# Retention in quarter-array blocks, heads kept at rows h//4, and a new place for the retention blocks and the sums in a fused retention and gated MLP kernel

## The chip, the cores and the metric

The kernel runs on one core of one Trainium2 chip. A core has a matrix engine (TensorE, "PE" in the profile; its weight loads are "PEld"), a vector engine (VectorE, "DVE"), a scalar engine (ScalarE, "ACT"), a general engine (GpSimd, "POOL") and a queue engine (SyncE, "SP") that issues most DMAs. Matmul results go to PSUM, which this kernel divides by names: `a`, `b` and `m` are two banks each, `n` and `st` one bank each, eight in all. A bank holds 2 KB for each of the 128 partitions.

The metric is the device time of one execution in microseconds, lower is better. Times are compared as the median of several runs, and the profile shows one of those executions.

## What is computed

Eight sequences of 576 positions, eight heads of 64. A retention block (attention without softmax, with a decay per head) is followed by an MLP with the activation h cos(h). All inputs and the output are float32; the kernel computes its matmuls in bfloat16 and sums in float32.

```
scale = 1.0 / np.sqrt(D_)
scores = scale * np.matmul(q, k.transpose(0, 1, 3, 2))
gamma = 1.0 - 2.0 ** (-5.0 - np.arange(H, dtype=np.float32))
Dmat = np.where(rel >= 0, gamma[:, None, None] ** rel[None, :, :], 0.0)
attn_out = np.matmul(scores * Dmat[None, :, :, :], v)

x = attn_out.transpose(0, 2, 1, 3).reshape(B * S, H * D)   # 4608 x 512
h = x @ w_in                                               # 512 -> 2048
out = (h * np.cos(h)) @ w_out                              # 2048 -> 512
```

## The kernel before

**Row blocks and tiles.** The 4608 token rows are 36 row blocks g of 128. Nine row blocks hold two sequences (1152 = 2 x 576 rows), so g % 9 says where a block lies: 0 starts a sequence, 4 (`MIX`) has the end of one sequence in its first 64 rows and the start of the next in the others, 8 ends one. The MLP works on ten tiles n of 512, 256, 256 and then seven times 512 rows. Tiles n = 3 (`S7`) to 9 (`last`) are the ones in which the second matmul is done by seven products instead of eight.

**Retention of a row block.** The decay splits into a factor for q rows and one for k rows, so `prep` (L128) multiplies q and k by tables (`gq`, `gk`, made by exponentials at the start) and casts v, mostly on POOL. The results are transposed, by TensorE for the first row blocks and by DMA later. Then, for eight heads written as pairs (head 2*hg + he, with he choosing one half of 128 partitions):

- `scores` (L176): eight matmuls of k rows against q rows, contraction 64, output 128 rows, into bank `a` or `b`, he in one or the other of its two banks; DVE multiplies by a causal mask and writes `ret` in bfloat16 (L192).
- `states` (L229): the sum over the block of k times v, eight matmuls of 128x64 per block, in two column halves; DVE adds the running state (`s`, L265, or a copy at a sequence start, L263), and `copy` (L251) casts it into one of four blocks `sb` (L256), block-diagonal 128x128 tiles with the two heads of a pair on the diagonal and zeros elsewhere.
- `attn_out` (L271): for two row blocks at a time, first the carried part, four full 128x128 matmuls of `sb` against q for each block (L283; not for a block that starts a sequence, and 64 columns for MIX), then the block's own part, eight matmuls of 128x64 of v against `ret` (L296); ScalarE casts the sum from bank `m` into the activations `xT` (L308).
- `state` and the single-block calls of `attn_out` do the same for the first row blocks.

**The MLP of a tile.** `mm1` (L312) makes h in eight blocks i = 0 to 7 in banks `a`, `b`, `m`; ScalarE computes cos(h) as a shifted sine (L331), DVE multiplies (L332) into `gT`. For n < 3, `mm2` accumulates 16 matmuls (L340) for each 128 rows. For n >= 3, gT and w_out are seen as 2 x 2 quarters and `mm2_seven` (L474) computes seven products of quarter sums, in the order 3, 4, 5, 2, 1, 7, 6 (called M3, M4 and so on here), each of 16 matmuls with 256 columns (L455). The sums of gT quarters (gs5, gs2, gs1, gs7, gs6) are made by `g_sum` (L383), each in two halves of four of eight blocks, on DVE or POOL; a POOL sum that follows a DVE one waits for it ("port free"). Sums of weight quarters are made once by `w_sums`. `sums_after` (L414) says after which mm1 block each sum is issued: for most tiles the first halves after block 3, the second after block 7.

M3, M5, M1 and M6 use bank `n`, M4, M2 and M7 bank `st`: M5 accumulates on M3 and M2 on M4, after the earlier value has been read out. The output quarters are combined by DVE (L484), collected in `pend` and issued by `flush` at the next product.

**The order.** Everything is in a hand-written order (`manual_schedule`): each engine executes its own instructions strictly in the order in which the code issues them, and semaphores are put in between from the tiles that they read and write. Retention work of later row blocks is put between the products: `unit7` (L711) issues, for two row blocks, states (bank `b`), the pending combination (`then`), attn_out (bank `m`), scores of the next two blocks (`scores2`, banks `a` and `b`) and the sb copies on ScalarE. The table `at` (L768) says ahead of which product a unit stands: M5 and M1 in tiles 5 to 8; in tiles 3 and 4 only scores ahead of M5, and units ahead of M1 and M6. `feed` (called at every store) issues the next preparations, transposes and loads.

Of the kernel before, what the change touches and what calls it, by code (L numbers as in the profile page):

```python
# [8 lines left out]
F32 = mybir.dt.float32  # L9
# [8 lines left out]
def kernel(  # L18
# [17 lines left out]
    P = 128  # L36
# [61 lines left out]
    blocks4 = [consts.tile([P, HG, P], BF16, tag=f"sb{x}", name=f"sb{x}") for x in range(4)]  # L98

    tiles = {}  # L100

# [26 lines left out]
    def prep(g, early=False):  # L128
# [6 lines left out]
        tq = gq[:, c, :].unsqueeze(2).to_broadcast([P, H, D])  # L135
        tk = gk[:, c, :].unsqueeze(2).to_broadcast([P, H, D])
        if not early:
            fq = tiles.pop(("fq", g))
            nc.gpsimd.tensor_tensor(out=qks[:, 0], in0=fq, in1=tq, op=ALU.mult)  # L139
        (nc.vector if g == 3 else nc.gpsimd).tensor_tensor(  # L140
            out=qks[:, 1], in0=fk, in1=tk, op=ALU.mult
        )
        if early:
            tiles["fv", g] = fv
        else:
            copy_v = nc.scalar.copy if g > starts[S7] // P + 17 else nc.gpsimd.tensor_copy
            copy_v(vb, fv)  # L147
            if c == MIX and g > PER:
                copy_v(v_odd[HP:, g // PER % 2], fv[HP:])
        qT = qT4[:, :, g * P : (g + 1) * P] if early else qkT[:, :HG, :]  # L150
# [25 lines left out]
    def scores(g, bank, idle=0):  # L176
# [3 lines left out]
        for hg in range(HG):  # L180
            for he in range(2):
                d0 = he * D
                nc.tensor.matmul(  # L183
                    ps[:, he, hg, :],
                    lhsT=qkT[d0 : d0 + D, HG + hg, :],
                    rhs=qT[d0 : d0 + D, hg, :],
                    start=True,
                    stop=True,
                )
        ret = retp.tile([P, 2, HG, P], BF16, tag="ret", name="ret")  # L190
        mask = tri_mix if g % PER == MIX else tri
        nc.vector.tensor_tensor(  # L192
            out=ret.rearrange("p a b i -> p (a b) i"),
            in0=ps.rearrange("p a b i -> p (a b) i"),
            in1=mask.unsqueeze(1).to_broadcast([P, H, P]),
            op=ALU.mult,
        )
        tiles["ret", g] = ret

    def state(g):  # L200
# [10 lines left out]
        for hg in range(HG):  # L211
# [3 lines left out]
                rhs=vs[p0:, 2 * hg : 2 * hg + 2, :].rearrange("s h d -> s (h d)"),  # L215
# [13 lines left out]
    def states(gs, bank="st"):  # L229
# [6 lines left out]
        ps = psum.tile([P, len(gs), HG, D], F32, tag=bank, name="st")  # L236
        for x, g in enumerate(gs):
            qks, vb, qkT, qT = tiles["a", g]
            vs = v_odd[:, g // PER % 2] if g % PER == MIX else vb
            for hg in range(HG):  # L240
                for he in range(2):
# [3 lines left out]
                        rhs=vs[:, 2 * hg + he, :],  # L245
                        start=(x == 0 and hg == 0),
                        stop=(x + 1 == len(gs) and hg == HG - 1),
# [3 lines left out]
        def copy(run=nc.vector.tensor_copy):  # L251
            for g in gs:
                s, sb = tiles.pop(("s32", g)), blocks4[g % 4]
                for he in range(2):
                    r = slice(he * D, he * D + D)
                    run(sb[r, :, r], s[r])  # L256
                tiles["sb", g + 1] = sb
# [13 lines left out]
    def attn_out(gs, bank, evac=nc.vector.tensor_copy):  # L271


        ps = psum.tile([P, len(gs), HG, P], F32, tag=bank, name="ov")
        for x, g in enumerate(gs):
            c = g % PER
            if c == 0:
                continue
            qT = tiles["a", g][3]
            sb = tiles.pop(("sb", g))  # L280
            n = HP if c == MIX else P
            for hg in range(HG):
                nc.tensor.matmul(  # L283
                    ps[:, x, hg, :n],
                    lhsT=sb[:, hg, :],
                    rhs=qT[:, hg, :n],
                    start=(hg == 0),
                    stop=False,
                    skip_group_check=True,
                )  # L290
        for x, g in enumerate(gs):
            vb = tiles["a", g][1]
            ret = tiles.pop(("ret", g))
            for hg in range(HG):
                for he in range(2):
                    nc.tensor.matmul(  # L296
                        ps[he * D : he * D + D, x, hg, :],
                        lhsT=vb[:, 2 * hg + he, :],
                        rhs=ret[:, he, hg, :],
                        start=(g % PER == 0 and hg == 0),  # L300
                        stop=(hg == HG - 1),
                        skip_group_check=True,
                    )
        n = max(m for m in range(len(starts)) if starts[m] <= gs[0] * P)
        if ("x", n) not in tiles:
# [3 lines left out]
            tiles["x", n][:, :, t0 : t0 + len(gs) * P].rearrange("p c (x i) -> p x c i", i=P), ps  # L309
# [73 lines left out]
    def g_sum(n, x, e0, e1):  # L383
# [9 lines left out]
        if ("gs", n, x) not in tiles:  # L393
# [4 lines left out]
        on_dve = x == 5 or (n, x) in ((S7, 1), (S7, 2)) or (n, x, e0) in (  # L398
            (last, 1, 0), (last, 2, 4), (S7 + 1, 2, 4)
# [14 lines left out]
    def sums_after(n, i):  # L414

        if n == S7:
            if i < 4:
                w_sums(3 + i % 2, i // 2 * 4, i // 2 * 4 + 4)
            if i == 6:
                g_sum(n, 5, 0, 4)  # L420
            elif i == 7:
                g_sum(n, 5, 4, E2)
                g_sum(n, 2, 0, E2)
                g_sum(n, 7, 0, 4)
        elif i in (3, 7):
            for x in (5, 2, 1, 7, 6) if n < last or i > 3 else (5, 1, 2, 7, 6):
                g_sum(n, x, i - 3, i + 1)

# [36 lines left out]
    def more_sums(n):  # L465

        if n == S7:
            g_sum(n, 7, 4, E2)
            prep_next()
            g_sum(n, 1, 0, E2)  # L470
            for e in (0, 4):
                g_sum(n, 6, e, e + 4)

    def mm2_seven(n, at):  # L474
# [21 lines left out]
        for x in (3, 4, 5, 2, 1, 7, 6):  # L496
            if x in at:
                at[x](flush)
# [326 lines left out]
```

## Time and profile before

| | us |
|---|---|
| median of 5 runs | 304.89 |
| the five runs | 303.71, 303.98, 304.89, 306.76, 309.3 |
| the profiled execution | 303.71 |
| its span, first to last instruction | 302.0 |
| mean granted TensorE clock | 0.994 |
| busy in one tile, 166.0 to 196.2 us: PE, DVE, ACT, POOL | 30.20, 21.23, 17.98, 25.06 |
| the same, 226.3 to 256.5 us | 30.20, 21.31, 16.94, 21.15 |
| busy from 134 to 152 us (tile n=4): PE, DVE, ACT, POOL | 17.07, 16.11, 6.86, 17.23 of 18.00 |

The page has, for every group of instructions, its source line, engine, operation, what it writes and reads, busy time and mean duration, then the idle time of the engine just before it and what ended that idle time. A duration of one matmul there contains its latency; because matmuls overlap, the cost of a group is read from the chain of work that ended last, in which the pieces add up to the time passed. In the timeline, a bracket at the end of a row is idle time before the row, with the instruction that ended it. Three rows of groups that the change touches, from the groups by shape (mean ns of one, idle before):

```
L242 PE MATMUL st<-vb,qks 128*64 128x64 bf16 x168 | 5.0, 198 | 0.4 <-DVE ret L192 0.4
L401 POOL TENSOR_TENSOR gs<-gT 128x1024 bf16<-128x1024 bf16 x49 | 104.8, 2174 | 44.4 <-DVE gs L401 44.4
L139 POOL TENSOR_TENSOR qks<-fq,gq 128x512 bf16<-128x512 f32 x32 | 34.6, 1082 | 39.2 <-DMA fq<-in_q_dram 35.1 <-PE o L340 4.1
```

### The profile page before, as it was taken

What the parts mean: (1) busy time and instruction counts of PE and PEld (TensorE: products, weight loads), DVE (VectorE), ACT (ScalarE), POOL (GpSimd) and SP (SyncE); (2) the same over time, 40 slices, a digit from 0 to 9 for tenths busy, and PEclk for the clock granted to TensorE, in tenths of its full rate; (3) what the DMA queues carried; (4) which work ended last, traced back from release to release, by engine and by line L of the source; (5) the groups of instructions that cost most, each with busy time, mean ns of one, the idle gap of its engine ahead of it and who ended that gap; (6) DMA issues with size and microseconds to landing.
All of it is one profiled execution on the core that took longest, in us unless ns stands there. A gap on an engine that the chain in (4) does not pass through costs nothing.

```text
span 302.0 us, 6662 instructions
## 1 busy us (share of the span) xinstructions
PE 292.1 (97%) x2761; PEld 200.7 (66%) x2761; DVE 209.5 (69%) x250; ACT 145.5 (48%) x187; POOL 199.0 (66%) x165
## 2 busy tenths in 40 slices
PE   8899999999999979998999999999999999999995
PEld 3478647758588867457754885488548854884594
DVE  6677647664689994589857874787488748835873
ACT  2656433515245352652466584648455645524620
POOL 2780067444445399989984998499849934970583
PEclk9999999999999998999999999999999999999999
DMA  7999999999989999999999997995860250022013
GB/s 207 212 210 207 203 199 210 208 252 176 233 176 213 209 213 219 226 244 194 204 242 184 247 231 143 229 210 143 171 142 2 72 139 2 0 72 69 2 35 104
DMA packets 154270, 50.23 MB, mean 166 GB/s; under 512 B 140801, under 2 KB 153217, under 8 KB 154241
## 3 DMA queue, kind: packets, MB, share of 16 engines
q1 hardware_dynamic: 150016, 45.63, 75.3%
q0 software_dynamic: 4224, 4.19, 8.4%
q8 instruction: 21, 0.34, 0.5%
q14 instruction: 9, 0.07, 0.1%
HBM read 36.70 MB, written 9.44 MB: 153 GB/s over the span
## 4 chain that ended last, share of the span: by engine, by line
PE 51%; DVE 1%; DVEq 0%; issue 0%
PE h L323 23%; PE o L455 22%; PE ov L296 2%; PE sc L183 2%; PE ov L283 2%; PE st L242 1%; DVE ret L192 1%; DVE ot L484 0%; DVEq L820 0%
## 5 line engine op out<-in xcount | busy, mean ns | idle before, releaser
L401 POOL TENSOR_TENSOR gs<-gT 128x1024 bf16<-128x1024 bf16 x49 | 104.8, 2174 | 44.4 <-DVE gs L401 44.4
L323 PE MATMUL h<-xT,w_in_sb 128*128 128x512 bf16 (+2 forms) x832 | 127.9, 313 | 0.9 <-DVE gT L332 0.4
L332 DVE TENSOR_TENSOR gT<-h,cosh 128x1024 bf16<-128x1024 f32 x72 | 87.9, 1223 | 43.6 <-ACT cosh L331 43.5
L331 ACT ACTIVATE cosh<-h,half_pi 128x1024 f32<-128x1024 f32 x72 | 80.2, 1113 | 64.7 <-PE h L323 62.7
L323 PEld LDWEIGHTS <-w_in_sb 128*128 128x128 bf16 x832 | 75.9, 98 | 50.2 <-issue 1.2
L455 PEld LDWEIGHTS <-gs 128*128 128x128 bf16 x576 | 54.7, 99 | 8.9 <-issue 0.6
L139 POOL TENSOR_TENSOR qks<-fq,gq 128x512 bf16<-128x512 f32 x32 | 34.6, 1082 | 39.2 <-DMA fq<-in_q_dram 35.1
L140 POOL TENSOR_TENSOR qks<-fk,gk 128x512 bf16<-128x512 f32 x35 | 37.3, 1066 | 10.0 <-DMA fk<-in_k_dram 9.5
L192 DVE TENSOR_TENSOR ret<-sc,tri 128x1024 bf16<-128x1024 f32 x32 | 38.0, 1219 | 3.9 <-PE sc L183 3.8
L455 PE MATMUL o<-ws,gs 128*128 128x256 bf16 (+1 forms) x352 | 40.0, 275 | 0.0
L484 DVE TENSOR_TENSOR ot<-o,ot 128x512 f32<-128x512 f32 (+2 forms) x32 | 19.7, 620 | 16.3 <-PE o L455 16.2
L340 PE MATMUL o<-w_out_sb,gT 128*128 128x512 bf16 x128 | 30.1, 380 | 0.0
L308 ACT CAST xT<-ov 128x1024 bf16<-128x1024 f32 (+1 forms) x18 | 16.5, 917 | 27.5 <-PE ov L296 27.3
L455 PE MATMUL o<-w_out_sb,gs 128*128 128x256 bf16 x224 | 25.8, 273 | 0.4 <-DVE ot L484 0.4
L455 PE MATMUL o<-w_out_sb,gT 128*128 128x256 bf16 x224 | 25.6, 273 | 0.0
L455 PEld LDWEIGHTS <-gT 128*128 128x128 bf16 x224 | 21.8, 98 | 3.9
L340 PEld LDWEIGHTS <-gT 128*128 128x128 bf16 x128 | 11.8, 98 | 12.6
L401 DVE TENSOR_TENSOR gs<-gT 128x1024 bf16<-128x1024 bf16 (+1 forms) x19 | 18.2, 974 | 0.4
L256 ACT CAST sb<-s 64x256 bf16<-64x256 f32 x40 | 16.1, 403 | 0.9 <-DVE s L263 0.4
L147 POOL CAST vb<-fv 128x512 bf16<-128x512 f32 x22 | 13.4, 610 | 3.0 <-DMA fv<-in_v_dram 2.8
L350 ACT COPY ot<-o 128x512 f32<-128x512 f32 x8 | 4.7, 589 | 17.1 <-PE o L340 17.1
L183 PEld LDWEIGHTS <-qkT 64*128 64x128 bf16 x288 | 8.2, 94 | 7.0 <-issue 3.4
(70 smaller groups left out, 178.2 us busy)
## 6 DMA issues: line engine op xcount, KB each, us to landing
out_dram<-ot SPq DMA_DIRECT2D x35, 256.0 KB, 3.4
fk<-in_k_dram SPq DMA_DIRECT2D x32, 256.0 KB, 5.0
fv<-in_v_dram SPq DMA_DIRECT2D x32, 256.0 KB, 5.2
fq<-in_q_dram SPq DMA_DIRECT2D x28, 256.0 KB, 4.4
w_in_sb<-in_moe_w_in_dram POOLq DMA_DIRECT2D x4, 512.0 KB, 8.9
w_out_sb<-in_moe_w_out_dram POOLq DMA_DIRECT2D x4, 512.0 KB, 16.3
fq<-in_q_dram SPq DMA_DIRECT2D x2, 512.0 KB, 4.3
fq<-in_q_dram SPq DMA_DIRECT2D x8, 128.0 KB, 4.1
```

What stands on the lines that cost most here:

```text
L139: nc.gpsimd.tensor_tensor(out=qks[:, 0], in0=fq, in1=tq, op=ALU.mult)
L140: (nc.vector if g == 3 else nc.gpsimd).tensor_tensor(out=qks[:, 1], in0=fk, in1=tk, op=ALU.mult)
L192: nc.vector.tensor_tensor(out=ret.rearrange("p a b i -> p (a b) i"), in0=ps.rearrange("p a b i -> p (a b) i"), in1=mask.unsqueeze(1).to_br ...
L256: run(sb[r, :, r], s[r])
L308: evac(tiles["x", n][:, :, t0 : t0 + len(gs) * P].rearrange("p c (x i) -> p x c i", i=P), ps)
L323: nc.tensor.matmul(ps[:, j, :], lhsT=w_in_sb[:, dg, (et + j) * P : (et + j + 1) * P], rhs=xT[:, dg, c0 : c0 + w], start=(dg == 0), stop=(d ...
L331: nc.scalar.activation(cosh, ps, ACTF.Sin, bias=half_pi, scale=1.0)
L332: nc.vector.tensor_mul(gT[:, et : et + m, c0 : c0 + w], ps, cosh)
L340: nc.tensor.matmul(ps, lhsT=gT[:, et, tsi * P : (tsi + 1) * P], rhs=w_out_sb[:, et, :], start=(et == 0), stop=(et == ET - 1),)
L401: i = (nc.vector if on_dve else nc.gpsimd).tensor_tensor(out=tiles["gs", n, x][:, e0:e1], in0=i0, in1=i1, op=op_)
L455: nc.tensor.matmul(dst[i], lhsT=lhs[:, e, j * P : (j + 1) * P], rhs=rhs[:, e, c0:c1], start=(x in (3, 4, 1, 7) and e == 0 and (i == 0 or l ...
L484: pend.append(lambda: nc.vector.tensor_tensor(out=out_, in0=in0, in1=in1, op=op_))
```

## The change

Heads are numbered differently inside the tiles: head h = 4*he + hg now lies at rows h//4 (the partition half he), column group hg, instead of head 2*hg + he. The products in `prep` write q and k in that order, and the first load of q is split over two queues to match. The output of attn_out is laid out as [P, 4, blocks, P] so that the row half he of a head decides its PSUM bank.

With it: the state copies become 128x64 tiles without zeros, so that the clearing of the four sb tiles falls away; the carried part is computed in matmuls of 64x64, one per head, and the own part comes ahead of it when two row blocks are done together; scores are computed in two parts of 64 output rows. A tile's first unit stands ahead of M4 instead of M5 (tiles 5 to 8), and its states go to bank `st`; those of the second, ahead of M1, to bank `n`. The second halves of the sums are issued behind the first unit's states (`late_sums`); in tiles 3 and 4 the sums have another order and other engines. The mask of a unit's second score bank can be put off behind the addition of M4.

```diff
-    blocks4 = [consts.tile([P, HG, P], BF16, ...) for x in range(4)]
+    blocks4 = [consts.tile([P, HG, D], BF16, ...) for x in range(4)]
+    def head(he, hg):
+        return he * HG + hg
...
-    def prep(g, early=False):
+    def prep(g, early=False, kv_first=False):
...
+        def scaled(eng, m, f, by):
+            eng.tensor_tensor(
+                out=qks[:, m].rearrange("p (b a) d -> p a b d", a=2),
+                in0=f.rearrange("p (a b) d -> p a b d", a=2),
+                in1=by[:, c, :].rearrange("p (a b) -> p a b", a=2).unsqueeze(3).to_broadcast(
+                    [P, 2, HG, D]
+                ),
+                op=ALU.mult,
+            )
...
-    def scores(g, bank, idle=0):
+    def scores(g, bank, idle=0, parts=1, put_off=None):
...
         for hg in range(HG):
-            for he in range(2):
-                d0 = he * D
-                nc.tensor.matmul(
-                    ps[:, he, hg, :],
-                    lhsT=qkT[d0 : d0 + D, HG + hg, :],
-                    rhs=qT[d0 : d0 + D, hg, :],
+            for i0 in range(0, P, P // parts):
+                for he in range(2):
+                    d0, i1 = he * D, i0 + P // parts
+                    nc.tensor.matmul(
+                        ps[i0:i1, he, hg, :],
+                        lhsT=qkT[d0 : d0 + D, HG + hg, i0:i1],
+                        rhs=qT[d0 : d0 + D, hg, :],
...
+        if put_off is None:
+            masked()
+        else:
+            put_off.append(masked)
...
     def states(gs, bank="st"):
...
-                for he in range(2):
-                    r = slice(he * D, he * D + D)
-                    run(sb[r, :, r], s[r])
+                run(sb, s)
...
     def attn_out(gs, bank, evac=nc.vector.tensor_copy):
+        two = len(gs) == 2
+        ps = psum.tile([P, DG, len(gs), P], F32, tag=bank, name="ov")
+        def out_of(h, x, n=P):
+            return ps[h % 2 * D : h % 2 * D + D, h // 2, x, :n]
+        def carried():
+            for h0 in (0, 2) if two else (0,):
+                for x, g in enumerate(gs):
...
+                    heads = [(he, h0 + j) for j in range(2) for he in range(2)]
...
+                    for he, hg in heads:
+                        h = head(he, hg)
+                        r = slice(he * D, he * D + D)
+                        k = r if two else slice(0, P)
+                        nc.tensor.matmul(
+                            out_of(h, x, n),
+                            lhsT=sb[k, hg, r] if sb.shape[2] == P else sb[k, hg, :],
+                            rhs=qT[k, hg, :n],
...
+        for part in (own, carried) if two else (carried, own):
+            part()
...
-        on_dve = x == 5 or (n, x) in ((S7, 1), (S7, 2)) or (n, x, e0) in (
-            (last, 1, 0), (last, 2, 4), (S7 + 1, 2, 4)
+        on_dve = x == 5 or (n, x) == (S7, 2) or (n, x, e0) in (
+            (S7, 1, 4), (last, 1, 0), (last, 2, 4)
         )
...
         if n == S7:
             if i < 4:
                 w_sums(3 + i % 2, i // 2 * 4, i // 2 * 4 + 4)
-            if i == 6:
-                g_sum(n, 5, 0, 4)
+            elif i < 6:
+                g_sum(n, 5, i % 4 * 4, i % 4 * 4 + 4)
+                if i == 5:
+                    g_sum(n, 6, 0, 4)
             elif i == 7:
-                g_sum(n, 5, 4, E2)
                 g_sum(n, 2, 0, E2)
-                g_sum(n, 7, 0, 4)
-        elif i in (3, 7):
-            for x in (5, 2, 1, 7, 6) if n < last or i > 3 else (5, 1, 2, 7, 6):
-                g_sum(n, x, i - 3, i + 1)
+                g_sum(n, 1, 4, E2)
+                g_sum(n, 1, 0, 4)
+                for e in (0, 4):
+                    g_sum(n, 7, e, e + 4)
+                prep_next(kv_first=True)
+                g_sum(n, 6, 4, E2)
+        elif n == S7 + 1 and i in (3, 7):
+            for x in (5, 2, 1):
+                g_sum(n, x, i - 3, i + 1)
+            for x in (7, 6) if i == 7 else ():
+                for e in (0, 4):
+                    g_sum(n, x, e, e + 4)
+        elif i == 3:
+            for x in (5, 2, 1, 7, 6) if n < last else (5, 1, 2, 7, 6):
+                g_sum(n, x, 0, 4)
+        elif i == 7 and n == last:
+            late_sums(n)
+    def late_sums(n):
+        for x in (5, 2, 1, 7, 6):
+            g_sum(n, x, 4, E2)
...
             elif x == 4:
-                add(u22, tiles["all", 4], u22)
+                pend.insert(0, lambda: nc.vector.tensor_tensor(
+                    out=u22, in0=tiles["all", 4], in1=u22, op=ALU.add
+                ))
...
     for h0 in (0, HG):
-        nc.sync.dma_start(
...
+        for a, queue in enumerate((nc.sync, nc.scalar)):
+            at = a * HG + h0 // 2
+            queue.dma_start(
...
-            for sb in blocks4:
-                nc.gpsimd.memset(sb, 0.0)
...
-    def scores2(g):
+    def scores2(g, put_off=None):
         if g < NG:
-            scores(g, "a")
-            scores(g + 1, "b")
+            scores(g, "a", parts=2)
+            scores(g + 1, "b", parts=2, put_off=put_off)
...
-        copy = states([g + 1, g + 2], "b")()
+        copy = states([g + 1, g + 2], bank)()
...
-                    5: lambda then: unit7(g, True, then),
-                    1: lambda then: unit7(g + 2, True, then),
+                    4: lambda then, off: unit7(g, "st", True, lambda: late_sums(n), off),
+                    1: lambda then, off: unit7(g + 2, "n", True, then),
...
-                        5: lambda then: (then(), scores2(g), more_sums(n)),
-                        1: lambda then: unit7(g, True, then),
-                        6: lambda then: unit7(g + 2, n > 3, then),
+                        5: lambda then, off: (then(), scores2(g)),
+                        1: lambda then, off: unit7(g, "n", True, then),
+                        6: lambda then, off: unit7(g + 2, "b", n > 3, then),
```

## The prediction

> **What bounds the kernel now.** I read the page's engine rows first, then the chain of work that ended last in order of time, then TensorE's waits, then the timeline around each wait. From the page:
>
> ```profile
> PE 292.1 (97%) x2761; PEld 200.7 (66%) x2761; DVE 209.5 (69%) x250; ACT 145.5 (48%) x187; POOL 199.0 (66%) x165
> PE 51%; DVE 1%; DVEq 0%; issue 0%
> ```
>
> TensorE is busy for 97% of the span, and the chain (followed back to 140 us) is TensorE almost alone. A gain must come from fewer TensorE nanoseconds or fewer TensorE waits. One whole tile (n=5) in the chain:
>
> ```profile
> 166.16 3.49 PE o L455 x32
> 169.65 0.37 PE st L242 x16
> 170.02 0.55 PE ov L283 x8
> 170.57 0.57 PE ov L296 x16
> 171.14 0.55 PE sc L183 x16
> 171.69 3.60 PE o L455 x32
> 175.29 0.37 PE st L242 x16
> ...
> 182.58 13.81 PE h L323 x64
> ...
> 205.77 0.33 PE ov L283 x4
> ```
>
> Columns: start, duration, instruction group. 32 product matmuls cost 3.49 us right after mm1 (109 ns each), but 3.60 us after the score matmuls: the change of array shape costs 0.11. In a unit the shape changes five times: full array, 128x64 (st), 128x128 (carried, L283), 128x64 (own, L296), 64x128 (scores), full array. Taking 0.10 to 0.11 off each piece leaves 0.44 us for eight carried matmuls (55 ns each), 0.46 for eight pairs of own blocks (57 ns a pair), 0.44 for eight pairs of scores (55 ns a pair), and 0.26 for eight pairs of st (32 ns a pair, 64 columns moving). So two half-array tiles do run together: a pair costs what one full matmul costs.
>
> TensorE's waits, and the timeline around them:
>
> ```profile
> PE sc L183 <- DVE s L265: 1.7, 1, 1.7
> PE o L455 <- DVE ot L484: 0.4, 1, 0.4
> PE st L242 <- DVE ret L192: 0.4, 1, 0.4
> ```
> ```profile
> 107.22 2.59 DVE L401 TENSOR_TENSOR gs<-gT 128x2048 bf16<-128x2048 bf16 x1
> ...
> 111.34 0.40 PE L183 MATMUL sc<-qkT 64*128 64x128 bf16 x8 [1.67 <-DVE s L265]
> ...
> 136.62 3.23 DVE L401 TENSOR_TENSOR gs<-gT 128x1024 bf16<-128x1024 bf16 x2
> ...
> 139.93 6.31 POOL L401 TENSOR_TENSOR gs<-gT 128x1024 bf16<-128x1024 bf16 x3 [0.63 <-DVE gs L401]
> 140.50 1.91 PE L455 MATMUL o<-w_out_sb,gs 128*128 128x256 bf16 x16 [0.43 <-DVE ot L484]
> ```
>
> All three waits are DVE running late behind gs sums, in tiles n=3 and n=4. In n=3 a 2.59 us sum stands ahead of the state additions, and the second score bank waits for them. In n=4 two sums take 3.23 us beside POOL's own.
>
> **The change part by part.** Let p be the price of a round of four quarter-array matmuls. No trace of before has such a round. From below p is 56 ns (the array is as full as with one 128-column matmul). The st pairs hint at more: four instructions (two weight loads, two matmuls) in 32 ns is 8 ns each, and a round has eight: 63 ns. From above it is 112 ns (only two run together). I take 63, the nearest row, and keep 56 and 112.
>
> (a) Carried blocks. Twelve pairs of row blocks lie in n=3 to 8. Before: seven full pairs at 0.44, three with a half-width MIX block at about 0.34 (the 0.45 rows less 0.11), two with a sequence start at 0.22 (the 0.33 row less 0.11): 4.54 us. After: four rounds for ten pairs, two for two pairs, 44 rounds: 2.77 us. Gain 1.77 (2.08 at 56).
>
> (b) Scores in two parts: twelve calls, 32 matmuls instead of 16, so eight rounds instead of eight pairs: 0.50 for 0.44. Loss 0.77 (0.10 at 56). The same array work in twice the instructions: it pays only through (c).
>
> (c) Shape changes. The new order st, own, carried, scores has the shapes 128x64, 128x64, 64x64, 64x64: three changes instead of five. Ten units with scores save two each, n=3's last saves one, n=8's last (neither states nor scores) gains one: 20 x 0.10 = 2.0 gained.
>
> (d) n=3. gs5's halves move to blocks 4 and 5; after the last cos product DVE has gs2 and half of gs1 (1.14 + 0.70, the price of such sums there), and the 2.59 us sum is gone. The 1.7 us wait goes. Late next: the states of the unit before M1 now write bank n, which M3 and M5 used, so they wait for DVE's u11 subtraction, queued behind u22's addition (0.68) and two masks (1.22 each). From 102.7 us on: 1.84 + 0.68 + 2.44 + 0.68 gives 108.3 against a want of 107.9, so 0.5 stays with the semaphore. And M4 needs the last two cos products, which two 0.7 us sums now precede; DVE is busy nine tenths there, and only the sb copies (four of 64 rows, 1.18 us, become two of 128) give some back: 0.5. Queued behind M4 are scores and M5. Net gain 0.8.
>
> (e) n=4. gs2's second half leaves DVE, so u22's addition comes some 1.5 us earlier and the waits before M2 and the first states (1.1 us with their sequencer part, plus 0.3 at 149.7) mostly go. But POOL, with six sums of 2.1 us from about 137.4, ends its last half of gs6 near 149.9, where M6 would read it near 149.3: 0.6 late, and M7's second half touches at 145.8. POOL's preparations queue behind. Gain 0.5.
>
> (f) New wait, n=5 to 8. States of the first unit write bank st, and M4 writes it next. In tile n=7 the last cos product ends at 228.82, two additions (0.89 us) end at 229.74, with 0.14 to TensorE's start (as at 111.2) 229.88. M3 ended near 227.98 and the shorter unit takes 1.72, so M4 could start at 229.70: 0.18 late, with M5 and M2 queued behind it. Three tiles with two additions: 0.55 lost. Elsewhere M4 is covered by the unit itself; were DVE another 0.5 us late, that comes on top in each of the four tiles. The gs5 half behind the additions ends near 230.6, M5's second half reads it after 232: covered. gs2's second half on POOL ends at 233.5 against a read at 234.2: covered by 0.6.
>
> (g) n=1 and 2, where attn_out comes ahead of states: five shape changes more (+0.5), carried rounds (-0.47), two score calls (+0.13): 0.15 lost.
>
> At nothing: the put-off mask (next read before M1, 1.7 us later), the half-size sb copies on ACT (0.40 each for 0.82, ACT 48% busy), the missing clears of sb (2.1 us of POOL at 19.3, then waiting for loads), and the first q loads over two queues (same bytes; ACT's two issues would cost it about 1 us, at SP's 0.5 each, ahead of an Exp that is needed at 4.7 and ended at 2.4). Without that cover each is worth its own price. SP's order behind those loads is the same, so later loads, transposes and stores move past nothing. The qks products in blocks of 64 have no row on POOL: the flat ones take 1.06 to 1.08. DVE's product over four dimensions takes 1.22 for 1024 elements, no more than a flat one, so I take no change. POOL has 9 us free in tile n=7 (21.15 of 30.2), so even 1.6 us each would be hidden there, though not in n=4.
>
> Sum: -1.77 +0.77 -2.0 -0.8 -0.5 +0.55 +0.15 = -3.6 us; at p=56, -4.6. The profiled execution took 303.71 (span 302.0, and 1.7 around it) and was the fastest of five, so it becomes 300.1. The median shown is 304.89, 1.2 higher; less 3.6 it is 301.3. I put the time at 300.6, between.
>
> **A rule against the change.** The Trainium skill, "TensorE: Matmul & The Clock Gate", section "Wait — 56ns, not 53.3ns?", says that the distance from one matmul start to the next never falls below about 25 ns, however short they are. Then a round of four costs 100 ns: (a) shrinks to 0.14, (b) costs 4.3, and the sum is +1.5 us, a slower kernel. The st row speaks against it: 16 matmuls in 0.26 us are 16 ns apart, weight loads included. The measurement decides, so 63 and not 100.
>
> **The rivals.**
>
> Quarters run two at a time (slower). A round costs 112 ns: (a) and (b) become -4.54+4.93 and +5.48, the sum +3.2, or 306.9 for the profiled execution and about 307.5 as a median. Place: scores and carried blocks of every unit from n=3 on. All 140 rounds together decide from p = 89 ns, where the sum is zero. For it: no trace shows four tiles at once. Against: rows and columns each pair freely, and the two row halves of scores and of carried blocks lie in different PSUM banks. Chance 0.1.
>
> DVE and POOL take the gain back (about the same). If M4 waits 0.5 us more in n=5 to 8, and n=3 and n=4 keep their waits, 2.0 + 1.3 go and 303.5 is left. For it: DVE at nine tenths before 103 us, POOL full in n=4. Against: in n=5 to 8 no other wait is within 0.5 us. Chance 0.22.
>
> All DVE waits go and p is 56: -4.6 -1.0 (d) -0.6 (e) -0.55 (f), or 297 profiled. Chance 0.2. The forecast itself: 0.48. That the shape changes do not fall away cannot be: the order of instructions alone gives the shapes.
>
> **How the numbers follow.** About 1% (3 us) is what a measurement of this kernel tells from no change. The forecast case lies at 1.2 to 1.5% and gives three quarters to faster, the rest to within 1%; the all-waits case is faster; the DVE case within 1%, the quarter case half and half. Faster 0.64, within 1% 0.29, slower 0.07. Range 296.8 to 304.2: from p=56 with no new wait to the DVE case as a median; the slower rival and a few tenths of the DVE case are left out.
>
> **What would show it.** Carried rows: 16 matmuls in about 0.35 us after a change, scores 32 in 0.50 to 0.55 with no change ahead of them. A tile of 30.2 us should become about 29.5. A wait of M4 (product line) on the state additions near 0.2 us; none of 1.7 us on the second score bank. Wrong if 32 scores take 0.8 us or more, or if a tile in n=5 to 8 shows waits of over 0.5 us.

## The result and the profile after

| | before | changed kernel |
|---|---|---|
| median, us (all executions) | 305.09 (301.85 to 310.59, 48) | 300.36 (298.49 to 305.25, 27) |
| ratio, 95% interval | | 0.988 (0.9854 to 0.9905) |
| profiled execution: time, span, granted clock | 303.71, 302.0, 0.994 | 303.77, 302.0, 0.989 |
| second profile of the same kernel: span, clock | 301.0, 0.994 | 297.7, 1.000 |

The changed kernel is 1.2% faster. Ratios, and medians by clock, here and below are of the fast executions alone, so 0.988 is not the quotient of the two medians (0.9845), and the profiled execution of the changed kernel is one of its slow ones. It has the same span as the one of before, so that pair says nothing until one knows where the two spend their time. The page of the changed kernel, engine row and the row of the granted clock (one digit for each fortieth of the span):

```profile
PE 289.6 (96%) x3113; PEld 197.2 (65%) x3113; DVE 209.7 (69%) x245; ACT 135.7 (45%) x167; POOL 199.4 (66%) x163
PEclk9999999999999999999999599999999999999999
```

TensorE still is the bound. The 5 stands at 166 to 173 us, in tile n=5. TensorE's timeline there, and then the stretch that follows (columns: stretch, length, then busy time and instructions of PE, PEld, DVE, ACT, POOL, then granted clock, DMA share, GB/s):

```profile
164.41 0.39 PE L195 MATMUL sc<-qkT 64*64 64x128 bf16 x16
168.57 0.64 PE L195 MATMUL sc<-qkT 64*64 64x128 bf16 x16 [3.77 <-DMA qkT<-qks]
```
```profile
168.50:173.70 5.20, 5.12 (x38) 3.67 (x39) 0.86 (x2) 0.00 (x0) 5.20 (x4) 0.50 1.29 254
```

The second score bank waits 3.77 us for a transpose by DMA, and from 1.6 us before the end of that wait TensorE runs at half clock for 6.8 us (167.0 to 173.8). A second profile, of another execution of the same kernel, has neither (span 297.7), and from here on I use it, called the second profile. In the profile of before the same kind of thing happens in tile n=3, after its wait of 1.67 us for the state additions (first fence, the products behind it; second fence, the stretch):

```profile
111.68 5.33 PE L455 MATMUL o<-ws,gs 128*128 128x256 bf16 x32
```
```profile
112.00:115.40 3.40, 3.40 (x18) 2.44 (x17) 2.39 (x3) 0.48 (x2) 3.40 (x3) 0.50 1.15 252
```

The 32 products take 5.33 us, where 3.67 is normal at full clock: 1.7 us is lost, directly behind the wait. The prediction read the wait just ahead of this row, and not the row.

Where the 4.3 us between the two spans (302.0 and 297.7) lie, from the starts of mm1 and of M3:

| stage, us | before | after | difference |
|---|---|---|---|
| up to M3 of n=3 | 100.13 | 100.20 | +0.07 |
| n=3, M3 to the next mm1 | 20.06 | 16.67 | -3.39 |
| n=4 | 31.99 | 32.21 | +0.22 |
| n=5, 6, 7, 8 | 30.23, 30.02, 30.23, 29.31 | 30.09, 29.69, 29.76, 29.09 | -0.14, -0.33, -0.47, -0.22 |
| tail, from the mm1 of n=9 | 30.04 | 29.94 | -0.10 |

Nearly all of it is n=3. Against the second profile of before (span 301.0) the other rows are the same within 0.02 us, but the first is 99.17 against 100.20: the changed kernel loses 1.0 us before n=3, and the gain between these two spans is 3.4. One unit in tile n=7 of the changed kernel, for the question whether the arrays do what was said (timeline of the first profile, whose long wait lies two tiles earlier; start, duration):

```profile
225.72 6.29 POOL L443 TENSOR_TENSOR gs<-gT 128x1024 bf16<-128x1024 bf16 x3
...
228.91 0.44 PE L266 MATMUL st<-vb,qks 128*64 128x64 bf16 x16
...
229.98 0.62 PE L195 MATMUL sc<-qkT 64*64 64x128 bf16 x32
...
230.35 2.21 DVE L443 TENSOR_TENSOR gs<-gT 128x1024 bf16<-128x1024 bf16 x1
...
230.53 1.92 PE L515 MATMUL o<-w_out_sb,gT 128*128 128x256 bf16 x16
...
232.28 1.91 PE L515 MATMUL o<-w_out_sb,gs 128*128 128x256 bf16 x16
...
233.62 0.68 DVE L557 TENSOR_TENSOR ot<-o,ot 128x512 f32<-128x512 f32 x1
...
234.35 1.91 PE L515 MATMUL o<-w_out_sb,gs 128*128 128x256 bf16 x16 [0.15 <-DVE ot L557]
```

The same places in before (timeline of n=7, where the unit stands ahead of M5; then POOL's row there, from a timeline of POOL alone):

```profile
228.85 0.80 DVE L401 TENSOR_TENSOR gs<-gT 128x1024 bf16<-128x1024 bf16 x1
...
229.83 0.44 PE L242 MATMUL st<-vb,qks 128*64 128x64 bf16 x16
...
231.88 3.67 PE L455 MATMUL o<-w_out_sb,gs 128*128 128x256 bf16 x32
```
```profile
226.96 4.67 POOL L401 TENSOR_TENSOR gs<-gT 128x1024 bf16<-128x1024 bf16 x2
```

Read the starts. From st to the product behind it the unit takes 1.62 us (228.91 to 230.53); before it took 2.05 (229.83 to 231.88). M4 does not wait. But further down stands something that the prediction had not: the gs5 half on DVE takes 2.21 us instead of 0.80, pushes the mask and the addition behind it, and M2 (234.35) starts 2.07 us after M5 (232.28), where 16 products take 1.75. TensorE's waits in the second profile (total, times, longest):

```profile
PE h L365 <- DVE gT L374: 1.7, 2, 1.3
...
PE o L515 <- DVE ot L557: 1.1, 4, 0.5
PE h L365 <- DVE xT L350: 0.7, 1, 0.7
...
PE sc L195 <- DMA qkT<-qks: 0.4, 1, 0.4
```

With the sequencer's part, M2 starts 2.41, 2.20, 2.07 and 2.07 us after M5 in n=5 to 8: 0.66, 0.45, 0.32 and 0.32 us of waits, 1.75 in four tiles. The gs5 half takes 2.56, 2.68, 2.22 and 2.22 us there.

### The profile page after: what moved, and what is told of

It is laid out like the page before. It is cut to its first block, busy times and chain, and to the rows that moved or that the text cites. A ratio compares the mean times of both kernels' runs of the same rounds, so it can differ in the third digit from the quotient of the medians.

```text
span 302.0 us, 7333 instructions
## 1 busy us (share of the span) xinstructions
PE 289.6 (96%) x3113; PEld 197.2 (65%) x3113; DVE 209.7 (69%) x245; ACT 135.7 (45%) x167; POOL 199.4 (66%) x163
## 5 line engine op out<-in xcount | busy, mean ns | idle before, releaser
L443 POOL TENSOR_TENSOR gs<-gT 128x1024 bf16<-128x1024 bf16 x51 | 106.9, 2126 | 42.9 <-DVE gs L443 42.9
L515 PE MATMUL o<-ws,gs 128*128 128x256 bf16 (+1 forms) x352 | 38.6, 268 | 0.0
L515 PE MATMUL o<-w_out_sb,gT 128*128 128x256 bf16 x224 | 28.2, 283 | 0.1
L515 PE MATMUL o<-w_out_sb,gs 128*128 128x256 bf16 x224 | 26.8, 276 | 0.6 <-DVE ot L557 0.6
L535 DVE TENSOR_TENSOR ot<-o,ot 128x512 f32<-128x512 f32 (+2 forms) x25 | 14.9, 603 | 13.5 <-PE o L515 13.4
L443 DVE TENSOR_TENSOR gs<-gT 128x1024 bf16<-128x1024 bf16 (+1 forms) x18 | 21.4, 1200 | 0.3
L195 PE MATMUL sc<-qkT 64*64 64x128 bf16 (+1 forms) x480 | 11.0, 220 | 4.7 <-DMA qkT<-qks 4.2
L195 PEld LDWEIGHTS <-qkT 64*64 64x64 bf16 (+1 forms) x512 | 9.1, 107 | 9.1 <-DMA qkT<-qks 4.5
```

What stands on the lines that cost most here:

```text
L195: nc.tensor.matmul(ps[i0:i1, he, hg, :], lhsT=qkT[d0 : d0 + D, HG + hg, i0:i1], rhs=qT[d0 : d0 + D, hg, :], start=True, stop=True,)
L443: i = (nc.vector if on_dve else nc.gpsimd).tensor_tensor(out=tiles["gs", n, x][:, e0:e1], in0=i0, in1=i1, op=op_)
L515: nc.tensor.matmul(dst[i], lhsT=lhs[:, e, j * P : (j + 1) * P], rhs=rhs[:, e, c0:c1], start=(x in (3, 4, 1, 7) and e == 0 and (i == 0 or l ...
L535: pend.append(lambda: nc.vector.tensor_tensor(out=out_, in0=in0, in1=in1, op=op_))
```

## The experiments

Ratios are to the kernel before, with 95% intervals.

**The changed kernel again**, unaltered.

> The changed kernel unaltered, for a second profile. Theory 1 (the transposes of row blocks 22 and 23 stand late in SP's queue, and the unit that now comes one product earlier in tile n=5 reaches them): the second score bank of n=5's first unit waits for a transposed tile again, between 0 and 4 us from run to run; the time is 0.985 to 0.990 of the kernel before. Theory 2 (the wait of 3.8 us in the first profile was a disturbance of that execution): no wait over 0.3 us there. In both, a carried group of 16 takes 0.35 us and M2 of n=6 to 8 waits 0.3 to 0.45 us for the addition of M4.

Measured: 299.36 us, ratio 0.9901 (0.9886 to 0.9917), span 297.7, full clock. It is the second profile above. The 3.77 us wait is absent, and SP's queue shows by how much (timelines of this profile, SP's issues and the scores that read the block):

```profile
159.90 1.39 SPq L167 DMA_TRANSPOSE qkT<-qks  x1
...
165.80 0.62 PE L195 MATMUL sc<-qkT 64*64 64x128 bf16 x32
```

The transpose is issued at 159.90 for scores at 165.80, 5.9 us later. In before it was issued at 163.10 for scores at 171.14, 8.0 us. In the first profile it was issued at 162.53, and TensorE stood ready at 164.8, only 2.3 us later: SP's queue was late there by 2.3 us at the transpose before already, and TensorE was 1.0 us earlier than here, since mm1 of n=4 had not waited. A transpose lands 4.2 to 5.0 us after its issue here. Scores now come some 5 us earlier (n=3 is shorter), the transposes come when SP's queue lets them: what was slack has become chance.

**Block 23's transpose earlier in SP's queue.**

```diff
-  ... + 4 * n + ((0, 1, 2, 4) if n else (-1, 0, 1, 4))[r]
+  ... + 4 * n + ((0, 1, 2, 4) if n > 1 else (1, 2, 2, 4) if n else (-1, 0, 1, 4))[r]
```

> In tile n=4 row blocks 22 and 23 are prepared and transposed one store earlier in SP's queue (about 6 us). Theory 1: the wait of n=5's second score bank for a transposed tile is gone or under 0.5 us, and the time falls to 0.978 to 0.985 of the kernel before, 1 to 3 us under the changed kernel, with less spread. Theory 2: the time stays within 0.3% of the changed kernel.

Measured: 299.87 us, 0.9907 (0.9883 to 0.9931), span 298.3. A miss: the edit moved the transpose past one store only (issued at 159.48), with the loads still ahead, and the unaltered kernel had no wait there in the same set of runs. It decides nothing.

**Carried blocks ahead of own**, which makes three shape changes five again.

```diff
-        for part in (own, carried) if two else (carried, own):
+        for part in (carried, own):
```

(The start and stop flags of the two parts move with it.)

> The carried part again ahead of the own part when two row blocks are done together. Theory 1 (a change of array shape costs 0.10 us by itself): st, carried, own, scores have two changes more in each of the ten full units, while the units of n=2, where states follow the own part, lose one each: 1.8 us slower than the changed kernel, and the chain shows own and scores pieces 0.10 us longer. Theory 2 (the gain of the order comes from the later need for the sb copies, not from the shapes): the pieces keep their lengths and a wait for a copy appears ahead of the carried part.

Measured: 299.89 us, 0.9919 (0.9904 to 0.9933), span 298.2. The unit in n=7 (timeline of this kernel):

```profile
224.86 0.44 PE L266 MATMUL st<-vb,qks 128*64 128x64 bf16 x16
...
226.72 1.92 PE L522 MATMUL o<-w_out_sb,gT 128*128 128x256 bf16 x16
```

224.86 to 226.72 is 1.86 us, 0.24 more than in the changed kernel, where two changes at the prediction's 0.10 to 0.11 make 0.20 to 0.22. The price of a shape change holds. But the whole kernel is only 0.5 us slower, not ten times 0.24 and not the 1.8 that was expected. The waits of M2 (L522) are gone from its list of waits, and the tiles n=6 and 7 are 0.24 longer (29.93 and 29.99), half of what their two units cost. TensorE that arrives later waits less: half of these nanoseconds had been turned into waiting in the changed kernel. The rest of the difference is waits that come and go: mm1 of n=4 does not wait here, and scores wait for transposes at 83, 166 and 174 us (1.72, 0.82, 0.25).

**Scores in one part instead of two.**

```diff
-            scores(g, "a", parts=2)
-            scores(g + 1, "b", parts=2, put_off=put_off)
+            scores(g, "a", parts=1)
+            scores(g + 1, "b", parts=1, put_off=put_off)
```

> Scores in one part (64x128, 16 matmuls for two blocks) instead of two, all else as changed. Theory 1 (a quarter round costs 63 ns, a pair 56 ns, a shape change 100 ns): the score piece is 0.06 us shorter but gets a shape change of 0.10 ahead of it, so 12 calls give +0.5 us, 0.1 to 0.2% slower than the changed kernel, hardly to be told from it; in the trace sc takes 0.55 with its change instead of 0.50. Theory 2 (starts at least 25 ns apart): 4 us faster than the changed kernel.

Measured: 298.9 us, 0.9897 (0.987 to 0.9924), span 297.4: no difference from the changed kernel. In the unit of n=7 the scores start 0.55 us ahead of M4 with either form (225.38 to 225.93 here, 229.98 to 230.53 in the fence above): eight rounds of four quarter tiles cost what eight pairs cost. The unit takes 1.72 us instead of 1.62, which is the one shape change more.

**The schedule alone, and the arrays alone.** The first keeps before's array shapes and row layout and takes the new order of sums, the order of units and products, the put-off mask. The second takes the quarter arrays and the rows h//4, and keeps before's sums, its bank b for state sums, and its places of the units.

```diff
-                        5: lambda then: (then(), scores2(g), more_sums(n)),
-                        1: lambda then: unit7(g, True, then),
+                        5: lambda then, off: (then(), scores2(g)),
+                        1: lambda then, off: unit7(g, "n", True, then),
```

(The core of the first; the second goes the other way.)

> The kernel before with the new schedule alone: units ahead of M4 and M1 in banks st and n, the new order and engines of the sums, the put-off mask; heads, copies, carried part, scores and order inside a unit as before. Theory 1 (the schedule removes the waits in n=3 and n=4 and brings the wait of M2 in n=5 to 8): -1.1 us in n=3, -0.6 in n=4, and M2 waits 0 to 0.3 us only, since the longer unit leaves DVE more time: 0.994 to 0.998 of the kernel before. Theory 2 (most of the gain is the schedule): 0.990 or less.

> The changed kernel with the old schedule: heads at rows h//4, copies of 128x64, own part first, quarter-array carried part and scores, but units ahead of M5 and M1 in bank b and the old sums. Theory 1 (a round of four costs 56 ns and a shape change 100): a unit costs 1.82 us instead of 2.25, together 4.0 us less, the wait of 1.8 us in n=3 stays, DVE's half of gs5 in n=5 to 8 takes 0.8 us and M2 doesn't wait: 0.985 to 0.989 of the kernel before, so as fast as the changed kernel or faster. Theory 2: 0.994 or more.

Measured: the schedule alone 300.6 us, 0.9884 (0.9829 to 0.9939), span 297.6. The arrays alone 301.66 us, 0.9957 (0.9939 to 0.9976), span 300.5. Both results fell on the side of the second theory: most of the gain is the schedule. The schedule alone in n=3 (timeline):

```profile
109.41 0.62 PE L185 MATMUL sc<-qkT 64*128 64x128 bf16 x16
109.97 3.67 PE L482 MATMUL o<-ws,gs 128*128 128x256 bf16 x32
```

No wait between the two score banks, 32 products in 3.67 us, clock 1.00. Its n=3 and n=4 are 2.45 and 1.02 us shorter than before; its tiles n=5 to 8 take what they took before (30.23, 29.99, 30.23, 29.31), although the gs5 half takes 2.2 to 2.7 us in them too: the longer unit hides it. The arrays alone, at the same place, and in n=7 (timeline):

```profile
106.92 2.60 DVE L443 TENSOR_TENSOR gs<-gT 128x2048 bf16<-128x2048 bf16 x1
...
111.06 0.42 PE L195 MATMUL sc<-qkT 64*64 64x128 bf16 x16 [2.03 <-DVE s L287]
111.41 5.33 PE L497 MATMUL o<-ws,gs 128*128 128x256 bf16 x32
...
230.01 0.86 PE L195 MATMUL sc<-qkT 64*64 64x128 bf16 x32
```

The 2.6 us sum, the wait (now 2.03) and the half clock are all there. Its tiles n=5 to 8 take 29.98, 29.60, 29.98, 29.03, only 0.25 to 0.42 less than before: TensorE reaches the second score bank sooner, and that bank still holds the state sums. In n=7 M5 starts 0.80 us after the scores (230.01 to 230.81) where 0.55 is the length without a wait, and it is 0.85 in the second unit, so 0.55 us of what the arrays save in this tile is waited away. So the schedule alone brings as much as the whole change. What the arrays add to it is not seen in the time, although each unit is shorter: the next experiment shows where it goes.

**POOL pauses before DVE's gs5 half.** The first half of gs6 moves from the middle of the tile to the end of its late sums, so that POOL is idle when DVE wants to start.

```diff
-            for x in (5, 2, 1, 7, 6) if n < last else (5, 1, 2, 7, 6):
+            for x in (5, 2, 1, 7) if n < last else (5, 1, 2, 7, 6):
                 g_sum(n, x, 0, 4)
...
-        for x in (5, 2, 1, 7, 6):
+        for x in (5, 2, 1, 7):
             g_sum(n, x, 4, E2)
+        for e in (0, 4) if n < last else (4,):
+            g_sum(n, 6, e, e + 4)
```

> The changed kernel with the first half of gs6 moved from behind block 3 to the end of the late sums in n=5 to 8, so that POOL has a pause when DVE makes the second half of gs5. Theory 1 (that DVE sum takes 2.2 to 2.7 us because it waits for the end of a running POOL sum; M2 then waits for the addition queued behind it): the sum takes 0.7 us, the waits of M2 (0.3 to 0.7 us in each of four tiles) fall under 0.1, and the time is 1.2 to 1.8 us under the changed kernel. Theory 2 (the sum is slow for another reason, such as the banks): the sum stays over 2 us and the time within 0.2% of the changed kernel.

Measured: 297.7 us, 0.9803 (0.975 to 0.9856), span 296.1. The gs5 half takes 0.68 us and M2's waits are gone; tiles n=5 to 7 take 29.43, 29.24, 29.44. Tile n=8 does not gain (29.24): there M6 waits about 0.45 us for POOL's later sums. With the pause in n=5 to 7 only:

> The changed kernel with POOL's pause in n=5 to 7 only, tile n=8 as changed: in n=8, whose last unit has no scores, M6 comes earlier and waited 0.4 us for the late gs6 when the pause held there too. Theory 1: tiles n=5 to 7 take 29.2 to 29.5 us, n=8 29.1 as in the changed kernel, and the time is 1.2 to 1.8 us under the changed kernel, 0.978 to 0.985 of the kernel before, so the version with the pause repeats. Theory 2 (the lower time with the pause came from that chip): 0.988 or more.

Measured: 297.62 us, 0.983 (0.9789 to 0.987), span 295.6; n=5 to 7 take 29.66, 29.24, 29.43 and n=8 29.10. The tile n=7 (timeline; the same places as in the long fence above):

```profile
224.19 0.68 DVE L443 TENSOR_TENSOR gs<-gT 128x1024 bf16<-128x1024 bf16 x1
...
224.95 8.38 POOL L443 TENSOR_TENSOR gs<-gT 128x1024 bf16<-128x1024 bf16 x4 [1.18 <-DVE gs L443]
...
226.12 3.66 PE L517 MATMUL o<-w_out_sb,gs 128*128 128x256 bf16 x32
```

M5 and M2 run through as one block of 32 products in 3.66 us. This is the version that beats both kernels: its interval lies below that of the changed kernel's repeat (0.9886 to 0.9917), and its median is 1.7 us under that repeat's 299.36.

**The kernel before once more**, for the half clock.

> The kernel before, unaltered, for a second profile. If the halved clock from 112.0 to 115.4 us in the first profile follows from the wait of 1.7 us ahead of it only now and then: the wait of the second score bank in n=3 is there again, 1.5 to 2 us, and with a granted clock of 1.0 the span is 300.2 to 300.6 us.

Measured: 302.77 us, span 301.0, clock 0.994. The half clock was there again, at 110.8 to 114.2 us, behind a wait of 1.68 us of the second score bank, so this profile does not show the kernel at full clock. But the half clock is not in every execution of it. Of the 68 executions of before that were timed beside these experiments, 41 have a granted clock of 0.997 or more (3.4 us at half clock in a span of 301 make 0.994). In three of the four sets their median is 0.3, 0.4 and 0.9 us below that of the executions near 0.994 (302.47 against 302.81, 302.33 against 302.72, 302.23 against 303.16; the fourth set has one execution to compare, and no difference). So of the 1.7 us that n=3 loses at half clock, 0 to 0.9 are seen in the time of the whole kernel. No profile shows an execution of before at full clock; the next experiment shows where such a gain can go.

**Before with n=3's new sums only.**

```diff
-            if i == 6:
-                g_sum(n, 5, 0, 4)
+            elif i < 6:
+                g_sum(n, 5, i % 4 * 4, i % 4 * 4 + 4)
+                if i == 5:
+                    g_sum(n, 6, 0, 4)
```

(With it goes the rest of n=3's new order: its other sums and the next block's preparation, behind the last block.)

> The kernel before with the new order and engines of the sums in tile n=3 alone; units, banks, arrays and all other tiles as before. Theory 1 (the 2.6 us sum of gs1 on DVE ahead of the state additions made the wait of 1.8 us and, through it, 3.4 us of halved clock): the wait of the second score bank falls under 0.6 us, the granted clock stays full from 108 to 118 us, and the time falls by 2 to 3.3 us to 0.989 to 0.994 of the kernel before. Theory 2 (the bank matters: states share bank b with the second scores): the wait stays over 1 us and the clock dips again, within 0.3% of the kernel before.

Measured: 302.7 us, 1.0001 (0.9973 to 1.003), span 300.2. In n=3 it does all it should: no wait of the second score bank, no half clock, 17.33 us for the products instead of 20.06. Then n=4 gives back a part (timeline of DVE and TensorE there):

```profile
133.25 4.28 DVE L403 TENSOR_TENSOR gs<-gT 128x1024 bf16<-128x1024 bf16 x2
...
138.19 1.91 PE L463 MATMUL o<-w_out_sb,gs 128*128 128x256 bf16 x16 [1.48 <-DVE ot L483]
```

Two DVE sums beside POOL's take 4.28 us where 1.4 would do, and M2 waits 1.48 instead of 0.43. Tile n=4 takes 33.03 us instead of 31.99 and n=5 30.71 instead of 30.23: 1.5 of the 2.7 us are given back. The rest is about the 1.7 of the half clock, which most executions of before do not have, and that fits a ratio of 1.00. In this kernel a gain ahead of n=4 was worth nothing as long as n=4's sums stayed where they were.

**n=4's first sums two blocks later**, in the changed kernel. There the gs5 half takes 2.89 us, shut out by three instructions of POOL's preparations (from 126.13, 127.13 and 128.12 on), and mm1 waits (second profile, timeline of n=4):

```profile
126.38 2.89 DVE L443 TENSOR_TENSOR gs<-gT 128x1024 bf16<-128x1024 bf16 x1
127.13 1.04 POOL L140 TENSOR_TENSOR qks<-fk,gk 128x512 bf16<-128x512 f32 x1
...
130.46 1.89 PE L365 MATMUL h<-xT,w_in_sb 128*128 128x512 bf16 x8 [1.34 <-DVE gT L374]
```

```diff
-        elif n == S7 + 1 and i in (3, 7):
-            for x in (5, 2, 1):
-                g_sum(n, x, i - 3, i + 1)
+        elif n == S7 + 1:
+            for x in (5, 2, 1) if i in (5, 7) else ():
+                g_sum(n, x, 2 * i - 10, 2 * i - 6)
```

> The changed kernel with the first halves of n=4's sums behind mm1 block 5 instead of 3, nothing else. Theory 1 (the DVE sum of 2.9 us behind block 3 is held up by POOL's preparations, and mm1 waits 1.3 us for the product behind it): the sum takes 0.7 us, the wait of mm1 is gone, and the time is 0.5 to 1.5 us under the changed kernel. Theory 2 (POOL's sums now start later and M7 or M6 wait for them): as much is lost there again, within 0.2% of the changed kernel.

Measured: 299.17 us, 0.9894 (0.9875 to 0.9913), span 298.0. The DVE sum takes 0.68 us and mm1's wait is gone, but POOL now ends its sums later and M7 waits 0.72 for them; n=4's products take 18.12 us instead of 16.89, and the tile 31.94 instead of 32.21. The wait was handed on.

**All of these at once**: the pause in n=5 to 7, n=4's later sums, a transpose ahead of three loads (with the edit of the second experiment), and in n=2 states ahead of attn_out again.

```diff
-            ahead = starts[S7] // P + 14 if n == 0 and r < 3 else prepared + LD
+            ahead = starts[S7] // P + 14 if n == 0 and r < 3 else prepared + LD - (n == 1 and r == 0)
...
-        attn_out([g, g + 1], bank, nc.scalar.copy)
         copy = states([g + 1, g + 2])()
+        attn_out([g, g + 1], bank, nc.scalar.copy)
```

> The changed kernel with four edits of order: first half of gs6 late in n=5 to 7 (POOL's pause), the first halves of n=4's sums behind block 5 instead of 3, row block 23's transpose ahead of three loads in SP's queue, and in n=2 states ahead of attn_out. Theory 1 (the array part is worth 0.8 us a tile and was hidden behind waits for DVE sums that a POOL instruction holds up): no wait of M2 over 0.1 us, n=4's first DVE sum 0.7 us and no wait of mm1 there, tiles n=5 to 7 at 29.4 us, a span of 294 to 295.3 us, 0.970 to 0.977 of the kernel before. Theory 2 (waits come back elsewhere): a span of 296 us or more, like the version with POOL's pause alone.

Measured: 298.39 us, 0.9874 (0.9855 to 0.9894), span 296.4, no better than the pause alone, as the second theory had it. A wait for a transpose in n=5 (0.46), a longer one at 83 us (0.87 instead of 0.40) and M7's wait for POOL (0.74) came in place of those removed.

## Why the prediction was right, and where it was not

The number was right, 300.6 against 300.36, and so was the direction. The terms behind it were not, and their errors cancel, which is luck: the mechanism that was to bring most of the gain, the arrays, brought little of it that shows in the time.

- **The price of a quarter round.** Predicted 63 ns, with 56 as the lower end. Four quarter tiles start 3 to 4 ns apart and eight rounds of scores take 0.45 us (229.98 to 230.53 less one shape change of 0.10): 56 ns, the lower end. The rival of quarters running two at a time falls: 32 scores would have taken 0.9. So does the sum by the 25 ns rule.
- **Shape changes.** Carried first cost 0.24 us for two changes: right. A full unit became 0.43 us shorter; the sum had 0.19 - 0.06 + 0.20 = 0.33. Two such units in a tile make 0.86, and from before to the version with the pause a tile gains nearly that (30.23 to 29.44 in n=7 is 0.79).
- **The new wait, n=5 to 8 (f): the step that failed.** The prediction had M4 late behind the state additions, 0.55 us in all, and called the gs5 half behind them "covered" at its old 0.80 us. M4 was never late. The gs5 half takes 2.2 us and more, because it now meets a POOL sum that is already running, and M2 waits 1.75 us in four tiles. The starts show it: before, DVE's sum began at 228.85 and a POOL sum ended near 229.1 (sums of 2.1 us from 226.96 on); after, DVE's sum is first in line at 230.35, in the middle of a POOL sum of about 229.9 to 232.0 (three sums from 225.72 in 6.29 us), and ends at 232.56. The Trainium skill states the mechanism. "SBUF — State Buffer", section "Terms", says that DVE and GpSimd share a pair of ports that one of them holds for a whole instruction while the other blocks. Section "Who interferes with whom" says that a DVE instruction with two SBUF inputs contends in this way with a GpSimd instruction that reads SBUF; the gs sums on both engines read both of their inputs from there. The runs agree: 2.21 us with POOL busy, 0.68 with POOL idle. What the tiles n=5 to 7 gained in the second profile (0.14, 0.33, 0.47) and what M2 waited there (0.66, 0.45, 0.32) make 0.80, 0.78 and 0.79 us, and with the pause these tiles gain 0.80, 0.78 and 0.79: the part of the saving that was missing had become M2's wait. The prediction even had the row 3.23 us for two sums in n=4, and didn't ask what the phase of POOL would be after the move.
- **n=3 (d).** Predicted 0.8 gained. The wait of 1.83 (1.67 in the list, the rest the sequencer's part) went, the two new waits came as foreseen but smaller (M4's products 3.96 instead of 3.68, states 0.26 late: 0.5 together, 1.0 foreseen), and with the wait went the half clock behind it, 1.7 us, which was nowhere in the sum. Arrays included n=3 gives 3.39. Between these two profiles this is the largest term, but more than half of the executions of before have no half clock and are only 0 to 0.9 us faster, so in the median the half clock is worth that and not 1.7.
- **n=4 (e).** Predicted 0.5 gained. M2's wait of 0.43 went, but mm1's of 1.34 came, and the tile is 0.22 longer. In the first profile, where POOL's preparations fell elsewhere, mm1 does not wait and the tile takes 30.68. This term is a matter of phase.
- **n=1 and 2 (g).** Predicted 0.15 lost, and 1.0 is lost against the second profile of before. Two waits make up most of it, and neither profile of before has them: mm1 of n=2 waits 0.69 for the cast of xT, and scores wait 0.40 for a transpose at 82 us. The first is in all nine profiles in which own blocks come ahead of carried ones, and in none of the five others, so the order that saves shape changes costs it here.
- **"Later transposes move past nothing."** True of SP's order, but wrong as a reason for no cost: the reader of the transposes moved, by about 5 us. In the first profile that went with a wait of 3.77 us and 6.8 us at half clock; in the later profiles of versions of the changed kernel this wait in n=5 is 0 to 0.8.
- **What was worth what.** The sum gave 3.0 to the arrays and 0.75 to the rest. Alone, the arrays give 0.4% and the schedule 1.2%, as much as both together. The arrays' nanoseconds are real but end in waits, for M2 above all; with the pause they come out, and the time goes to 297.6.

What stays open: whether transposes pushed further ahead in SP's queue would make the first profile's long wait rarer; the one edit made for it hardly moved them. It is no single case: 9 of the 28 executions in the first set of the changed kernel have a granted clock of 0.994 or less and take 302.4 to 305.3 us, the others 298.5 to 301.5, but only one of them has a trace. And the two profiles of before differ by 0.96 at M3 of n=3 (100.13 and 99.17), of which 0.6 is there at the first mm1 (18.43 and 17.80); why is not shown.

## What to carry to other kernels

When TensorE arrives sooner at everything, list for each wait behind the change the slack of its releaser, DMA queues among them: a gain that no releaser follows is a wait. Before calling a DVE instruction covered, look at what POOL runs at its new start, and price it by the row beside POOL, not by the one that was alone. A right total says little of its parts: one run with half the change either way shows which half earned it.

## What the runs showed of the hardware

- Waits of TensorE listed with 1.67, 1.68 and 2.03 us in n=3 (before twice, the arrays alone) were each followed by 3.4 us at half clock, which costs 1.7 more in that stage; with the one of 3.77 went 6.8 us. Waits of 1.34 and 1.48 were not, but neither was one of 1.72 at 83 us in the kernel with carried blocks first, and 41 of 68 other executions of before kept a clock of 0.997 or more. So length alone does not decide it, and what does stays open; in its stage such a wait may cost twice what the list of waits says, while whole executions of before at that clock took only 0 to 0.9 us longer.
- The DVE sum of 128x1024 bf16 operands takes 0.68 us with POOL idle and 2.2 to 2.9 when a POOL instruction has begun shortly before it (0.80 when a POOL sum is about to end). At 2.89 three POOL instructions that follow each other without a gap overlap it, and it ends 0.5 us after the last of them (129.27 against 128.73): DVE did not get in between them.
- Quarter-array matmuls of 128 columns start 3 to 4 ns apart within a round of four, and a round takes 56 ns, its weight loads included.
